# Turning x on VectorE by 32 x 32 blocks, with the product q (k^T v) on quarters of TensorE's columns

## The chip, the cores and the metric

One core of one Trainium2 chip. The metric is the device time of one execution in microseconds (us), lower is better. PE is TensorE's matmul side, DVE is VectorE, ACT is ScalarE.

## The reference

Linear attention with a norm over each head, then a two-layer network with a squared relu:

```python
kv  = einsum('bhsd,bhse->bhde', k, v)          # 8 batches, 8 heads, 576 positions, 64 wide
out = einsum('bhsd,bhde->bhse', q, kv)
x   = out / sqrt(mean(out*out, -1) + 1e-6) * g_norm
x   = x.transpose(0, 2, 1, 3).reshape(4608, 512)
h   = x @ w_in                                 # 512 x 2048
g   = s * maximum(h, 0)**2 + b
y   = g @ w_out                                # 2048 x 512
```

All of it is f32. The two large products dominate. They need x with its features on the partitions, that is, turned.

## The kernel before

The 4608 rows are 36 chunks of 128 tokens, four chunks to a unit, nine units. The large products run by one level of Strassen's scheme (line 84 is their one helper), in slots of 16 matmul records. While the second product of unit u runs, the attention of unit u + 1 is slipped in between its slots, a piece at a time. For each chunk: q is turned (`turn`), multiplied by the block-diagonal k^T v (`product`), normed (`norm`), and turned again (`turn_x`). The pieces that the change touches:

```python
def kv_product(b):                       # k^T v of one batch: 72 matmuls on 64 x 64 quarters
    ...
    nc.tensor.matmul(ps[r][l * HB : l * HB + HB, i, :],
                     lhsT=kv[rows, 0, l, j, :], rhs=kv[rows, 1, l, j, :], ...)
    ...
    nc.scalar.copy(to, ps[r][ls])        # out of PSUM into the block diagonal bd_kv

def product():
    for p in range(NP):                  # NP = 4 pairs of heads
        if b == b1:                      # a chunk of one batch: all 128 columns
            matmul(ps[:, p, :], st["qT"][:, p, :], bd_kv[b % 2][:, p, :], True, True)
            continue
        for s in range(2):               # 4 of 36 chunks: a half of the columns for each batch
            half = slice(s * HB, s * HB + HB)
            nc.tensor.matmul(ps[half, p, :], lhsT=st["qT"][:, p, half],
                             rhs=bd_kv[(b + s) % 2][:, p, :], start=True, stop=True)
    ...

def turn_x():
    ps = ps_t.tile([P, NP, P], FP32, name="xT_ps", tag="t")
    for p in range(NP):
        nc.tensor.transpose(ps[:, p, :], st["xn"][:, 2 * p : 2 * p + 2, :], ident)
    ...
    nc.scalar.activation(xT[u][:, :, j * P : j * P + P], ps, AF.Copy, scale=g_col)
```

## Time and profile before

| | before |
|---|---|
| median | 994.3 us |
| span of the profiled run | 992.7 us |
| TensorE busy | 98% |
| VectorE, ScalarE busy | 46%, 21% |
| turning x (four transposes a chunk, 36 chunks) | 2% of the chain that ended last |

TensorE sets the time nearly everywhere, so what counts is how long its instruction stream is. Durations in the profile are latencies of a pipeline that overlap: a record of the large products lasts 379 ns, but the next one starts 216 ns after it. So the length of the stream is read from starts. The prediction below shows the lines.

### The profile page before, as it was taken

How to read it: one execution, taken by the hardware profiler on the slowest of the kernel's cores; microseconds unless marked ns; L12 is line 12 of the kernel's file. 1: busy time of each engine (PE TensorE's matmuls, PEld its weight loads, DVE VectorE, ACT ScalarE, POOL GpSimd, SP SyncE). 2: the span in 40 equal slices, each digit the busy share in tenths (PEclk: the TensorE clock that was granted, in tenths of full speed). 3: DMA queues.
4: the chain of work that ended last, by engine and by line, in shares of the span. 5: the costliest groups of instructions: out<-in, count | busy, mean ns of one | idle time of the engine just before them, and what ended most of it. 6: DMA issues, size and time to landing. Idle time of an engine off the chain costs nothing.

```text
span 992.7 us, 13559 instructions
## 1 busy us (share of the span) xinstructions
PE 970.0 (98%) x5826; PEld 854.0 (86%) x5826; DVE 452.8 (46%) x741; ACT 203.7 (21%) x350; POOL 3.9 (0%) x12
## 2 busy tenths in 40 slices
PE   4999999999999999999999999999999999999998
PEld 4788788888888888888888888888888888888887
DVE  2789548452445334533345244523453344334431
ACT  2674131212121212121211212121212111112100
POOL 1000000000000000000000000000000000000000
PEclk9999999999999999999999999999999999999999
DMA  9679728522551345132543255226113340323033
GB/s 263 202 267 243 234 75 233 139 85 96 159 139 51 119 135 124 54 137 74 151 112 126 65 149 139 85 85 173 40 42 127 87 126 1 130 74 137 1 127 85
DMA packets 74028, 121.47 MB, mean 122 GB/s; under 512 B 41584, under 2 KB 47728, under 8 KB 66672
## 3 DMA queue, kind: packets, MB, share of 16 engines
q1 hardware_dynamic: 72208, 119.16, 39.9%
q10 hardware_dynamic: 1632, 1.44, 0.6%
q8 instruction: 46, 0.75, 0.3%
q14 instruction: 14, 0.11, 0.0%
q0 software_dynamic: 128, 0.00, 0.0%
HBM read 103.81 MB, written 16.78 MB: 121 GB/s over the span
## 4 chain that ended last, share of the span: by engine, by line
PE 95%; DVE 3%; DMA 1%; ACT 0%; issue 0%; SPq 0%; ACTq 0%; DVEq 0%
PE x_ps L84 51%; PE y_ps L84 30%; PE z_ps L84 8%; PE kv_ps L297 2%; PE qT_ps L327 2%; PE xT_ps L372 2%; DMA kv_sb<-in_v_dram 1%; DVE ws L186 1%; PE x_ps L345 0%; DVE xs L186 0%; DVE a L183 0%; DVE ws L183 0%; SPq L96 0%; DVE xn L363 0%; DVE a L426 0%
## 5 line engine op out<-in xcount | busy, mean ns | idle before, releaser
L84 PE MATMUL x_ps<-w_sb,a 128*128 128x256 f32 x768 | 172.3, 379 | 0.0
L84 PEld LDWEIGHTS x_ps<-w_sb,a 128*128 128x128 f32 x768 | 144.3, 190 | 18.9 <-issue 0.2
L84 PE MATMUL y_ps<-w_sb,a 128*128 128x256 f32 x640 | 143.4, 379 | 0.0
L84 PEld LDWEIGHTS y_ps<-w_sb,a 128*128 128x128 f32 x640 | 119.4, 190 | 15.2 <-issue 0.2
L84 PE MATMUL x_ps<-xs,ws 128*128 128x256 f32 x512 | 121.1, 379 | 1.3 <-DVE ws L186 1.1
L469 ACT COPY r<-x_ps 128x512 f32<-128x512 f32 x96 | 56.3, 586 | 315.4 <-PE x_ps L84 307.4
L84 PE MATMUL y_ps<-xs,wb 128*128 128x256 f32 x512 | 121.0, 379 | 0.0
L84 PEld LDWEIGHTS x_ps<-xs,ws 128*128 128x128 f32 x512 | 97.1, 190 | 15.2 <-issue 1.4
L84 PEld LDWEIGHTS y_ps<-xs,wb 128*128 128x128 f32 x512 | 97.3, 190 | 13.2
L183 DVE TENSOR_TENSOR a<-y_ps,r 128x512 f32<-128x512 f32 x64 | 44.0, 688 | 122.1 <-ACT r L469 122.1
L84 PE MATMUL x_ps<-xT,wa 128*128 128x256 f32 x384 | 91.1, 384 | 0.0
L84 PEld LDWEIGHTS x_ps<-xT,wa 128*128 128x128 f32 x384 | 74.1, 193 | 10.4
L426 DVE SCALAR_TENSOR_TENSOR a<-a 128x512 f32<-128x512 f32 x96 | 66.4, 692 | 3.3
L541 DVE SCALAR_TENSOR_TENSOR or<-x_ps,s_col,b_row 128x256 f32<-128x256 f32 x52 | 25.0, 482 | 91.4 <-PE x_ps L84 87.2
L84 PE MATMUL x_ps<-xT,ws 128*128 128x256 f32 x256 | 61.1, 381 | 0.0
L84 PE MATMUL z_ps<-xT,wa 128*128 128x256 f32 x256 | 60.5, 379 | 0.0
L84 PE MATMUL x_ps<-w_sb,s 128*128 128x256 f32 x256 | 57.8, 380 | 0.0
L356 DVE TENSOR_REDUCE ss<-xn 128x8 f32<-128x512 f32 x36 | 24.6, 684 | 71.8 <-ACT xn L354 71.8
L502 DVE TENSOR_TENSOR a<-a 128x512 f32<-128x512 f32 x32 | 22.2, 692 | 76.0 <-ACT a L501 76.0
L84 PEld LDWEIGHTS z_ps<-xT,wa 128*128 128x128 f32 x256 | 48.6, 190 | 6.6
L84 PEld LDWEIGHTS x_ps<-xT,ws 128*128 128x128 f32 x256 | 48.1, 190 | 6.7
L84 PEld LDWEIGHTS x_ps<-w_sb,s 128*128 128x128 f32 x256 | 47.6, 190 | 6.1 <-issue 0.2
(96 smaller groups left out, 835.7 us busy)
## 6 DMA issues: line engine op xcount, KB each, us to landing
w_sb<-w SPq DMA_DIRECT2D x56, 1024.0 KB, 4.9
out_dram<-o SPq DMA_DIRECT2D x72, 128.0 KB, 2.3
q_sb<-in_q_dram SPq DMA_DIRECT2D x70, 128.0 KB, 5.8
kv_sb<-in_k_dram SPq DMA_DIRECT2D x30, 288.0 KB, 5.3
kv_sb<-in_v_dram SPq DMA_DIRECT2D x30, 288.0 KB, 6.7
w_raw<-in_moe_w_in_dram SPq DMA_DIRECT2D x8, 1024.0 KB, 5.4
w_raw<-in_moe_w_out_dram SPq DMA_DIRECT2D x8, 1024.0 KB, 5.0
w<-w_up SPq DMA_DIRECT2D x3, 1024.0 KB, 7.1
```

Source lines behind the costliest of these rows:

```text
L84: nc.tensor.matmul(o, lhsT=lhsT, rhs=rhs, start=start, stop=stop, skip_group_check=True)
L183: nc.vector.tensor_tensor(out=o, in0=a, in1=b, op=ALU.add)
L186: nc.vector.tensor_tensor(out=o, in0=a, in1=b, op=ALU.subtract)
L297: nc.tensor.matmul(ps[r][l * HB : l * HB + HB, i, :], lhsT=kv[rows, 0, l, j, :], rhs=kv[rows, 1, l, j, :], start=(j == 0), stop=(j == R - 1),)
L327: nc.tensor.transpose(ps[:, p, :], q_in[c][:, 2 * p : 2 * p + 2, :], ident)
L356: nc.vector.reduce_sum(st["ss"], st["xn"], axis=mybir.AxisListType.X)
L372: nc.tensor.transpose(ps[:, p, :], st["xn"][:, 2 * p : 2 * p + 2, :], ident)
L426: nc.vector.scalar_tensor_tensor(t, t, 0.0, t, ALU.max, ALU.mult)
L469: nc.scalar.copy(st[name], src)
L502: nc.vector.tensor_mul(t, t, t)
L541: nc.vector.scalar_tensor_tensor(o, ps, s_col, other, ALU.mult, ALU.add)
```

## The change

The intent is to take the four transposes of x in each chunk off TensorE and give them to VectorE, which has room. VectorE's transpose turns only blocks of 32 x 32 (the page is named in the prediction). The new layout takes each block to stay on its 32 partitions. So the product writes each block of 32 tokens of a head pair to the quarter of the partitions on which its features shall lie, and k^T v's columns, w_in's rows and g_norm are put in an order that fits. ScalarE then scales by g_norm in place.

```diff
@@ load of w_in
-  in_=src.rearrange("(c p) n -> p c n", p=P)[...]
+  in_=src.rearrange("(p c) n -> p c n", c=KC)[...]
@@ g_norm: 8 small loads in place of 2
-  for l in range(2): ... g_col[l * HB : l * HB + HB, :] <- g_norm "(p o) -> p o"
+  for h in range(H): ... g_col[h * e : h * e + e, :] <- g_norm "(e c) -> e c"
@@ kv_product: v is streamed in the new order of columns
-  ps[r][l * HB : l * HB + HB, i, :],
+  ps[r][l * HB : l * HB + HB, i, :].rearrange("p (c e) -> p c e", c=KC),
-  rhs=kv[rows, 1, l, j, :],
+  rhs=kv[rows, 1, l, j, :].rearrange("p (e c) -> p c e", c=KC),
@@ product: quarters of the columns, neighbours on different quarters
+  for w in range(4):
+      for p in range(NP):
+          nc.tensor.matmul(ps[32 * p : 32 * p + 32, w, :],
+                           lhsT=st["qT"][:, p, 32 * w : 32 * w + 32],
+                           rhs=bd_kv[(b if w < 2 else b1) % 2][:, p, :], start=True, stop=True)
@@ norm: writes runs of 16 elements
@@ turn_x
-  4 x nc.tensor.transpose(...); nc.scalar.activation(xT[...], ps, AF.Copy, scale=g_col)
+  nc.vector.transpose(out=to, in_=st["xn"]...)
+  every second chunk: 4 x nc.scalar.activation(to[:, i], to[:, i], AF.Copy, scale=g_col[:, i : i + 1])
```

More of the change, by code (lines that the diff above doesn't have):

```diff
@@ L136, in load_w @@
                 out=dst.rearrange("p (c n) -> p c n", c=KC),
-                in_=src.rearrange("(c p) n -> p c n", p=P)[:, :, f * n : f * n + 2 * n],
+                in_=src.rearrange("(p c) n -> p c n", c=KC)[:, :, f * n : f * n + 2 * n],
             )
@@ L266 @@
         nc.gpsimd.memset(t, 0.0)
-    g_col = const.tile([P, 1], FP32, name="g_col")
-    for l in range(2):
+    g_col = const.tile([P, KC], FP32, name="g_col")
+    for h in range(H):
+        e = D // KC
         nc.gpsimd.dma_start(
-            out=g_col[l * HB : l * HB + HB, :], in_=g_norm.rearrange("(p o) -> p o", o=1)
+            out=g_col[h * e : h * e + e, :], in_=g_norm.rearrange("(e c) -> e c", c=KC)
         )
@@ L338, in product @@
                 ps = ps_a.tile([P, NP, P], FP32, name="x_ps", tag="x")
-            for p in range(NP):
-                if b == b1:
-                    matmul(ps[:, p, :], st["qT"][:, p, :], bd_kv[b % 2][:, p, :], True, True)
-                    continue
-                for s in range(2):
-                    half = slice(s * HB, s * HB + HB)
+            for w in range(4):
+                for p in range(NP):
                     nc.tensor.matmul(
-                        ps[half, p, :],
-                        lhsT=st["qT"][:, p, half],
-                        rhs=bd_kv[(b + s) % 2][:, p, :],
+                        ps[32 * p : 32 * p + 32, w, :],
+                        lhsT=st["qT"][:, p, 32 * w : 32 * w + 32],
+                        rhs=bd_kv[(b if w < 2 else b1) % 2][:, p, :],
                         start=True,
@@ L362, in norm @@
             nc.vector.reciprocal(inv, rms)
+            shape = (P, H, KC, D // KC)
             nc.vector.tensor_tensor(
-                out=st["xn"], in0=st["x"], in1=inv.unsqueeze(2).to_broadcast((P, H, D)),
+                out=st["xn"].rearrange("p h d -> p (h d)").rearrange(
+                    "p (c h e) -> p h c e", c=KC, h=H
+                ),
+                in0=st["x"].rearrange("p h (c e) -> p h c e", c=KC),
+                in1=inv.unsqueeze(2).unsqueeze(3).to_broadcast(shape),
                 op=ALU.mult,
@@ L369, in turn_x @@
             u, j = divmod(c, 4)
-            ps = ps_t.tile([P, NP, P], FP32, name="xT_ps", tag="t")
-            for p in range(NP):
-                nc.tensor.transpose(ps[:, p, :], st["xn"][:, 2 * p : 2 * p + 2, :], ident)
             if j == 0:
                 xT[u] = xp.tile([P, KC, 2 * TB], FP32, name="xT", tag="xT")
-            nc.scalar.activation(xT[u][:, :, j * P : j * P + P], ps, AF.Copy, scale=g_col)
+            to = xT[u][:, :, j * P : j * P + P]
+            nc.vector.transpose(
+                out=to, in_=st["xn"].rearrange("p h d -> p (h d)").rearrange("p (c x) -> p c x", c=KC)
+            )
+            if j % 2 == 1:
+                to = xT[u][:, :, j * P - P : j * P + P]
+                for i in range(KC):
+                    nc.scalar.activation(
+                        to[:, i], to[:, i], AF.Copy, scale=g_col[:, i : i + 1]
+                    )
         return turn, product, norm, turn_x
```

## The prediction

> **What bounds the kernel now.** I read the page's first two parts, then the chain that ended last, then the groups by form, and last the timeline of TensorE around the lines that the change touches.
>
> ```profile
> PE 970.0 (98%) x5826; PEld 854.0 (86%) x5826; DVE 452.8 (46%) x741; ACT 203.7 (21%) x350; POOL 3.9 (0%) x12
> ...
> PE 95%; DVE 3%; DMA 1%; ACT 0%; issue 0%; SPq 0%; ACTq 0%; DVEq 0%
> PE x_ps L84 51%; PE y_ps L84 30%; PE z_ps L84 8%; PE kv_ps L297 2%; PE qT_ps L327 2%; PE xT_ps L372 2%; DMA kv_sb<-in_v_dram 1%; DVE ws L186 1%; PE x_ps L345 0%; DVE xs L186 0%; DVE a L183 0%; DVE ws L183 0%; SPq L96 0%; DVE xn L363 0%; DVE a L426 0%
> ```
>
> TensorE is the bound in every stage but the first 35 us; VectorE is busy 46% and ScalarE 21%, so both have room on average. The part to be removed, the turning of x (L372), is about 2% of the chain. Its groups, with the other attention work on TensorE:
>
> ```profile
> L372 PE MATMUL xT_ps<-ident,xn 128*128 128x128 f32 x144 | 21.7, 273 | 1.9 <-DVE xn L363 1.7
> L297 PE MATMUL kv_ps<-kv_sb 64*64 64x64 f32 x1152 | 21.0, 231 | 11.4 <-DMA kv_sb<-in_v_dram 11.4
> L345 PE MATMUL x_ps<-bd_kv,qT 128*64 128x128 f32 x64 | 4.4, 279 | 0.0
> ```
>
> The durations (273 ns) are latencies of a pipeline; the cost is the spacing of starts. That is read in TensorE's timeline: first a chunk of 128 tokens that lies over two batches (product on halves of the columns), then an ordinary one:
>
> ```profile
> 328.85 0.60 PE L372 MATMUL xT_ps<-ident,xn 128*128 128x128 f32 x4
> 329.38 1.09 PE L345 MATMUL x_ps<-bd_kv,qT 128*64 128x128 f32 x16
> 330.41 3.72 PE L84 MATMUL y_ps<-w_sb,a 128*128 128x256 f32 x16
> ...
> 337.86 0.60 PE L372 MATMUL xT_ps<-ident,xn 128*128 128x128 f32 x4
> 338.29 1.06 PE L84 MATMUL x_ps<-bd_kv,qT 128*128 128x128 f32 x8
> 339.19 0.60 PE L84 MATMUL x_ps<-w_sb,s 128*128 128x256 f32 x2
> ```
>
> The reader is to see starts: ordinary, four transposes take 338.29 - 337.86 = 0.43 us and eight records of the product (four f32 matmuls, two records each) 0.90. Both are 0.11 us a record. The product on halves needs sixteen records of the same 128 columns, and from transposes to the next group it takes 330.41 - 328.85 = 1.56 against 339.19 - 337.86 = 1.33, and the group behind it takes 3.72 instead of the 3.62 that the same form takes elsewhere. So halves do run two at a time, and going into and out of that mode costs 0.23 + 0.10 = 0.33 us.
>
> The product k^T v already runs on 64 x 64 quarters:
>
> ```profile
> 276.28 1.89 PE L84 MATMUL x_ps<-xT,wa 128*128 128x256 f32 x8
> 278.10 2.33 PE L297 MATMUL kv_ps<-kv_sb 64*64 64x64 f32 x144
> 280.36 1.99 PE L84 MATMUL x_ps<-xT,ws 128*128 128x256 f32 x8
> ```
>
> 144 records in 280.36 - 278.10 = 2.26 us are 0.0157 us each. A 256-column record takes 0.216 (16 in 3.45 by the chain), so 64 columns alone would take 0.054: four tiles run at once.
>
> **What the Trainium skill says.** "TensorE: Matmul & The Clock Gate", Part 3: small matmuls whose outputs lie in different groups of 32 partitions run concurrently. The trace agrees for two column tiles and for four 64 x 64 tiles (above); four tiles of 32 columns are not in it. "TensorEngine Tiling (Array Packing)", Key Properties: a change of tiling mode drains TensorE. The trace agrees: 0.33 us there and back. "SBUF — State Buffer", Specifications: SBUF has lines of 16 bytes and wants at least two hits on a line for full bandwidth. No instruction of this trace streams with a stride, so nothing confirms or refutes it. "VectorE: DVE Perf Modes", The three transpose paths: VectorE turns only blocks of 32 x 32, to SBUF. The trace of before has none.
>
> **The change part by part.** There are 36 chunks; 4 run in the opening, 32 beside the large matmuls, 4 of these on halves already.
>
> 1. Removed from TensorE: four transposes a chunk, 32 x 0.436 = 14.0 us on the path (all 36: 15.7). This is the most that can be won: 1.6%.
>
> 2. The product now has sixteen matmuls, 32 records, on four column groups, in an order in which neighbours differ in group. Serial, 32 x 0.109 = 3.5 us; four at a time, 0.87, as before. Into and out of the mode: 0.33 by the halves, say 0.35. For 28 ordinary chunks that is new, 28 x 0.35 = 9.8 us. The 4 on halves pay it already: about 0.
>
> 3. Steady sum: -14.0 + 9.8 = -4.2 us. Most of the gain goes back to mode changes.
>
> 4. k^T v streams v with a stride of 4 f32, 16 bytes, so each element lies in a line of its own. If the stream keeps its rate: 0. If it halves, the 1.95 us of each batch (2.26 less some 0.3 of mode change) doubles: seven batches and the half of the first that isn't hidden by its loads, 7.4 x 1.95 = 14.4 us, all on the path.
>
> 5. VectorE gets one transpose of 128 x 512 a chunk. No duration is shown; I take the 0.69 us of its other one-element-a-cycle operations of that size (rows of L356, L363), 36 x 0.69 = 25 us, to 48% busy. The norm writes runs of 16 elements, at the same cost. ScalarE exchanges one 128 x 512 eviction (688 ns) for two in-place scalings of 128 x 256; a scaled 128 x 256 took 474 ns (L574), so about +0.26 us a chunk and a block of four of some 1.8 us per two chunks. Both hide in steady units: a chunk's product has two slots of 3.45 us till the next one.
>
> 6. In the first unit's second half products follow each other after one slot (5.2 us apart). There the block of four scalings stands in ScalarE's queue before the square of the next product; by adding up the queue I get VectorE's norm done 5.8 us after the slot's end where TensorE wants the bank at 5.1: one stall of 0.7 us.
>
> 7. The opening is a chain of latencies. The first large matmul started at 28.50, held by VectorE's copies. In the new order on VectorE two transposes of 0.69 stand among them, then the four scalings: the second transpose ends at 28.6, the scalings at 30.3, so +1.8 there. The next block's weights are prepared behind those and come at 35.1 against the 34.88 at which TensorE used them. The third block needs chunks 2 and 3 turned and scaled, 39.8 against 38.34: +1.5 stays.
>
> 8. g_norm is loaded in eight small DMAs instead of two. The order with its waits shows that b's load now waits for the second of them; b landed at about 12.1 us (issue at 3.93, 8.2 to landing), and VectorE's first operation waits for it. Landing at 10 for that one and some 4 to 7 us more gives 14 to 17, and VectorE is wanted at 16.4 (the copy of k^T v). I put 0.3 us. The other order of w_in's rows leaves size and number of pieces as they are: 0.
>
> Sum without the stride's cost: 994.3 - 4.2 + 0.7 + 1.6 + 0.3 = 992.7. With it: 1007.
>
> **Rivals.** (a) The stride costs. For it: the skill's line rule, every element on its own line. Against: f32 streams at one element per two array cycles (0.216 us for 256), half the rate of access that a 2-byte type would ask, and the 64 x 64 mode already reads two streams from each row without loss. I give it 0.4, and 1003 to 1010 us. (b) The four column groups don't run at once, for instance since f32 takes two records and both need the same tile. For it: nothing but that no such mode is in the trace. Against: halves and quarters do, with f32. It would cost 36 x 1 to 2.6 us, 1030 to 1085: 0.05. (c) Mode changes cost nothing here, since the removed transposes stood on the other side: 983. Against it, L345 shows the cost each of the four times with transposes before it: 0.05. (d) VectorE or ScalarE become the bound in the steady part: they would have to run over 3.4 us late in a slot; 48% and some 22% busy speak against it.
>
> **Range and chances.** The case without stride cost stands at 992.7, with 988 to 997 for the opening and the mode change; the other at 1007. The middle of the whole is a little over the first: 995. A range of 988.5 to 1009 holds both. Faster by over 2% would mean under 974.4, 20 us, more than the 15.7 that are taken away: 0.01. Slower by over 2% means over 1014, which needs (b) or a stride that costs more than half the rate: 0.06.
>
> **What would show it.** The product's line, formerly two forms, should have 1152 records, starts from product to next group 0.9 + 0.23 us apart in all chunks, and the next group lengthened by 0.10. kv_ps should keep 2.26 us per batch; at 4.2 rival (a) is right. The transposes of VectorE should be about 0.69 us, VectorE about 48% busy. The first large matmul should start near 30.3 us instead of 28.5. Wrong would be: a product of 3.5 us, a wait of TensorE for ScalarE's scaling or for xn in units after the first, or VectorE's first operation after 17 us.

## The result, and the profile after

The changed kernel takes 1002.0 us at the median (1001.6 to 1002.5, 4 runs) against 994.3 (994.1 to 994.6, 4 runs): ratio 1.0077, 95% interval 1.006 to 1.0095. It is within 2%, but clear of noise: the change loses 8 us, though it takes 14 us of work off TensorE.

The page of the changed kernel, engine totals and chain:

```profile
PE 979.1 (98%) x6514; PEld 851.7 (85%) x6514; DVE 474.6 (47%) x777; ACT 208.7 (21%) x386; POOL 6.7 (1%) x18
...
PE x_ps L84 48%; PE y_ps L84 30%; PE z_ps L84 8%; PE x_ps L345 3%; PE kv_ps L299 3%; PE qT_ps L331 1%; DMA kv_sb<-in_k_dram 1%; DMA q_sb<-in_q_dram 1%; DVE ws L186 1%; DVE xs L186 0%; DVE a L183 0%; DVE ws L183 0%; DVE a L437 0%; PE y_ps L345 0%; DVE wb L186 0%
```

The line of xT_ps is gone from the chain; kv_ps has gone from 2% to 3% of it, and the product has a line of its own with 3%. Neither VectorE nor ScalarE has become busy. The groups that take these places, by form:

```profile
L345 PE MATMUL x_ps<-bd_kv,qT 128*32 128x128 f32 x1088 | 37.3, 278 | 1.6 <-DVE qT L334 1.1 <-DVE xn L364 0.5
L299 PE MATMUL kv_ps<-kv_sb 64*64 64x64 f32 x1152 | 35.8, 293 | 10.2 <-DMA kv_sb<-in_v_dram 10.2
```

kv_ps has the same count of records as before, 1152, and 35.8 us busy where it had 21.0. TensorE's timeline around one batch's k^T v:

```profile
277.81 1.89 PE L84 MATMUL x_ps<-xT,wa 128*128 128x256 f32 x8
279.63 4.41 PE L299 MATMUL kv_ps<-kv_sb 64*64 64x64 f32 x144
283.97 2.00 PE L84 MATMUL x_ps<-xT,ws 128*128 128x256 f32 x8
```

From 279.63 to 283.97 are 4.34 us; before it was 2.26. And around an ordinary chunk's product:

```profile
329.32 3.62 PE L84 MATMUL x_ps<-w_sb,a 128*128 128x256 f32 x16
332.87 1.08 PE L345 MATMUL x_ps<-bd_kv,qT 128*32 128x128 f32 x32
333.88 3.72 PE L84 MATMUL y_ps<-w_sb,a 128*128 128x256 f32 x16
337.44 0.60 PE L331 MATMUL qT_ps<-ident,q_sb 128*128 128x128 f32 x4
```

32 records take 333.88 - 332.87 = 1.01 us where 8 took 0.90, so four column groups do run at once. But the group in front takes 332.87 - 329.32 = 3.55 where sixteen such records take 3.45, and the one behind is lengthened from 3.62 to 3.72: 0.11 + 0.10 + 0.10 = 0.31 us that an ordinary chunk did not pay before.

To see where all of the span went, I summed the intervals from the start of each matmul record to the start of the next, charged to the earlier one (us; the k^T v of the first batch falls into the first 40 us):

| charged to | before | after | e1 | e7 |
|---|---|---|---|---|
| turning x | 14.25 | 0 | 0 | 0 |
| k^T v, 7 batches | 15.87 | 30.37 | 15.85 | 16.31 |
| product | 29.09 | 32.35 | 32.35 | 30.14 |
| turning q | 14.03 | 14.14 | 14.14 | 14.38 |
| large products | 874.66 | 878.90 | 879.77 | 874.91 |
| first 40 us, and the end | 44.82 | 44.93 | 44.92 | 44.76 |
| span | 992.7 | 1000.7 | 987.0 | 980.5 |

(e1 and e7 are experiments below. The cut at 40 us falls into a group, so the last two rows can trade some records of 0.22 us.) Between before and after: -14.25 for turning, +14.50 for k^T v, +3.26 for the product, +4.24 for the large products, +0.2 for the rest: +8.0, the difference of the spans.

### The profile page after: what moved, and what is told of

Its sections match the earlier page's. It is cut to its first block, busy times and chain, and to the rows that moved or that the text cites. A ratio compares the mean times of both kernels' runs of the same rounds, so it can differ in the third digit from the quotient of the medians. Undisturbed runs are those within 1.5% of the kernel's fastest.

```text
span 1000.7 us, 15059 instructions
## 1 busy us (share of the span) xinstructions
PE 979.1 (98%) x6514; PEld 851.7 (85%) x6514; DVE 474.6 (47%) x777; ACT 208.7 (21%) x386; POOL 6.7 (1%) x18
## 4 chain that ended last, share of the span: by engine, by line
PE 94%; DVE 3%; DMA 2%; issue 0%; SPq 0%; ACT 0%; DVEq 0%; ACTq 0%
PE x_ps L84 48%; PE y_ps L84 30%; PE z_ps L84 8%; PE x_ps L345 3%; PE kv_ps L299 3%; PE qT_ps L331 1%; DMA kv_sb<-in_k_dram 1%; DMA q_sb<-in_q_dram 1%; DVE ws L186 1%; DVE xs L186 0%; DVE a L183 0%; DVE ws L183 0%; DVE a L437 0%; PE y_ps L345 0%; DVE wb L186 0%
```

## The experiments

The theory: streaming v with a stride of 16 bytes halves the rate of k^T v and costs 14.5 us; the changes into and out of the column mode cost 0.31 us in each of 28 chunks, 8.7; together they eat the 14.25 that the removal of the transposes brings. The rivals: that quarters or VectorE's transposes carry the loss; that any pattern other than contiguous slows the stream; that the cost at the products is of the work and not of the change of mode.

**e1: v contiguous, the order made in the eviction.** The changed kernel with (cut to its core; the output pattern and VectorE's copies for the first batch are changed alike)

```diff
-  rhs=kv[rows, 1, l, j, :].rearrange("p (e c) -> p c e", c=KC),
+  rhs=kv[rows, 1, l, j, :],
+  to = to.rearrange("p i (c e) -> p i c e", c=KC)
+  ev = ps[r][ls].rearrange("p i (e c) -> p i c e", c=KC)
-  nc.scalar.copy(to, ps[r][ls])
+  nc.scalar.copy(to, ev)
```

> The changed kernel with v streamed contiguously; its columns are put in the new order when k^T v is copied out of PSUM instead. Theory (the 16-byte stride of the moving operand costs 14.5 us): kv_ps back to 2.26 us per batch, 1002.0 - 14.5 = 987.5, which is faster than the kernel before by 7 us. Rival (the product on quarters or the VectorE transposes carry the loss): it stays near 1002. If the permuted eviction is slow on ScalarE it is still hidden, since the copies are off the chain.

Correct, 987.7 us (986.7 to 988.8, 5 runs), ratio 0.9930 to before (0.9917 to 0.9944). The group of kv_ps is what it was before:

```profile
L299 PE MATMUL kv_ps<-kv_sb 64*64 64x64 f32 x1152 | 21.0, 231 | 11.0 <-DMA kv_sb<-in_v_dram 11.0
```

So all of the 14.5 us hang on how v is read, and without them the kernel is 7 us faster than before. (Some 1.6 of these 7 us are a pause that the kernel before has and e1 has not; see e2.) The eviction reads PSUM with the stride now, and ScalarE's copies took 259 ns in the mean where they took 260: the order costs nothing there.

**e2, e3, e4: the kernel before, with only v's stride.** In each, v is streamed with a stride of 4, 2 or 8 f32 and the order is undone in the eviction, so the results are right (the diff is cut in the same way):

```diff
-  rhs=kv[rows, 1, l, j, :],
+  rhs=kv[rows, 1, l, j, :].rearrange("p (e c) -> p c e", c=4),      # e3: c=2, e4: c=8
+  ev = ps[r][ls].rearrange("p i (c e) -> p i e c", c=4)             # undone
```

> The kernel before with only v streamed with a stride of 4 f32 (16 bytes), and the order undone in the eviction, so the result is right. Theory: kv_ps 4.3 us per batch and 994.3 + 14.5 = 1008.8. Rival (kv_ps was slow in the changed kernel by something else, such as the loads' timing): 994.

> The kernel before with v streamed with a stride of 2 f32 (8 bytes), undone in the eviction. If what counts is two hits on a 16-byte line: kv_ps stays 2.26 us per batch and the time 994.3. Rival (any step over one element, or the two-dimensional pattern itself, costs): kv_ps 3.3 to 4.3 us, 1001 to 1009.

> The kernel before with v streamed with a stride of 8 f32 (32 bytes), undone in the eviction. If each 16-byte line that is opened for one element costs the same: as with 4, kv_ps 4.3 us per batch, 1007. If the cost grows with the distance: more, 1020 and up.

All correct. Stride 4: 1006.9 us (4 runs), ratio 1.0127 (1.0113 to 1.0141). Stride 2: 994.5 (4 runs), 1.0001 (0.9987 to 1.0014). Stride 8: 1006.9 (one run). The group of kv_ps, in the order 2, 4, 8, each from its own run:

```profile
L297 PE MATMUL kv_ps<-kv_sb 64*64 64x64 f32 x1152 | 21.1, 230 | 10.9 <-DMA kv_sb<-in_v_dram 10.9
```

```profile
L297 PE MATMUL kv_ps<-kv_sb 64*64 64x64 f32 x1152 | 35.8, 293 | 10.8 <-DMA kv_sb<-in_v_dram 10.8
```

```profile
L297 PE MATMUL kv_ps<-kv_sb 64*64 64x64 f32 x1152 | 36.2, 295 | 10.5 <-DMA kv_sb<-in_v_dram 10.5
```

A stride of 8 bytes is free, 16 bytes costs 14.7 us of busy time more, and 32 bytes hardly more than that. It is the step that the line rule cited in the prediction leads one to expect: two elements on a 16-byte line are enough, one is not. The pattern's being two-dimensional, which e3 has too, is not the cause. All of this is f32 on 64 x 64 quarters; no run strides the operand of a matmul on the whole array. The time of e2 rose by 12.7 us and not by 14.5. In its trace a pause is missing that the trace of before has in the first unit:

```profile
114.09 0.92 PE L84 MATMUL x_ps<-w_t,a 128*128 128x256 f32 x3
116.47 1.78 PE L84 MATMUL x_ps<-w_t,a 128*128 128x256 f32 x7 [1.46 <-issue]
```

TensorE stands idle for 1.5 us in the middle of a group (1.84 us from start to start where 0.22 is usual, so 1.6 are lost), waiting for nothing that the profile shows. e3 has a shorter one at the same record (1.2 lost); the changed kernel and the traces of all other experiments have none. With it, 14.5 - 1.6 = 12.9 fits the 12.7.

No experiment was made on the pause, but the packets in the traces point at the instructions' own loads. Queue q8 brings instructions in blocks of 16 KB, 46 of them before and 51 after, in step with TensorE's 5826 and 6514 matmul records. Before, such a block starts at 114.12 us and TensorE goes on at 116.47; in e3 they are at 113.59 and 115.90, so both go on 2.3 us after the block's start. In e2 and e4 the same block starts at 114.04 and 113.12, while the slower k^T v still runs (until 116.36 and 115.3), and there is no pause. In the changed kernel no block starts between 97.02 and 117.71. So TensorE may have run out of instructions behind the quick k^T v; this fits and is not shown.

**e5 and e5b: the kernel before with all products on halves.** This leaves the transposes where they were and measures the change of mode alone:

```diff
-  if b == b1:
+  if False:
       matmul(ps[:, p, :], ...)
```

> The kernel before with all products on halves of the columns, as it has them for 4 of 36 chunks. Nothing else changes, so it measures the mode change alone. By the prediction's 0.33 us a chunk: 28 x 0.33 = +9.2, 1003.5. By what the changed kernel's intervals give (about 7.0 us for 28 chunks): 1001. If mode changes were free: 994.3.

The first try gave a wrong result (1001.2 us, ratio 1.0070, 1.0056 to 1.0083): I had overlooked that the second half then reads `bd_kv[(b + s) % 2]`, the other batch's matrix. Put right (`b if s == 0 else b1`):

> The run e5_halves put right: there the second half of the tokens read the k^T v of the other batch, so its result was wrong. Theory: correct, and the same time, 1001, with L345 and what is around it 0.31 us longer per chunk; if the wrong matrix had brought a wait of its own, less than 1001.

Correct, 1001.6 us (one run), so the wrong matrix had not changed the time. Its timeline around an ordinary chunk:

```profile
329.44 0.60 PE L372 MATMUL xT_ps<-ident,xn 128*128 128x128 f32 x4
329.97 1.09 PE L345 MATMUL x_ps<-bd_kv,qT 128*64 128x128 f32 x16
330.99 3.72 PE L84 MATMUL y_ps<-w_sb,a 128*128 128x256 f32 x16
```

0.53 from the transposes to the product where the ordinary chunk of before had 0.43, 1.02 to the next group against 0.90, and 3.72 against 3.62: 0.32 us, the same as with quarters. Over 28 chunks 9.0, less the pause of 1.6 that this trace lacks too, gives 7.4; measured 1001.6 - 994.2 = 7.4.

**e6: e1 with neighbours on the same quarter.**

```diff
-  for w in range(4):
-      for p in range(NP):
+  for p in range(NP):
+      for w in range(4):
```

> e1 with the two loops of the product exchanged, so that four neighbours go to the same column group. If neighbours must differ in group to run at once (matmuls start in program order): some 3.5 us a chunk in place of 0.9, 32 to 36 x 2.6 = +83 to +94 us, 1071 to 1081. If TensorE looks further ahead: 988.

Correct, 1033.2 us (one run): both numbers missed, though the direction was that of the first. One product:

```profile
326.71 3.62 PE L84 MATMUL y_ps<-w_sb,a 128*128 128x256 f32 x16
330.26 2.46 PE L347 MATMUL x_ps<-bd_kv,qT 128*32 128x128 f32 x32
332.65 3.72 PE L84 MATMUL x_ps<-w_sb,a 128*128 128x256 f32 x16
```

2.39 us in place of 1.01. Strictly one after the other, 32 records of 0.109 would be 3.5. If each started in program order, only the last record of a quarter could run beside the first of the next, an estimate of 29 x 0.109 = 3.2. The single records in the trace show more overlap: the first record of a quarter lasts 297 ns and those behind it some 273, and such a first record starts at 330.73, just after the fifth of the eight on the quarter before it (330.72; told apart by their spacing of 0.11), whose last three start later, at 330.83, 330.94 and 331.05. So TensorE looks ahead, not far. The order that the change chose, neighbours on different quarters, is worth 1.4 us a chunk.

**e7: e1 with two products back to back.** If the cost at the products is that of going into and out of the mode, two chunks can share it. The product of every second chunk gets a bank of the pool that the transposes of x no longer use:

```diff
-  product = [whole(*steps) for steps in zip(product, norm)]
+  pair = [[product[i], product[i + 1], norm[i], norm[i + 1]] for i in (0, 2)]
-  ps = ps_a.tile([P, NP, P], FP32, name="x_ps", tag="x")
+  pool, tag = (ps_t, "t") if c % 2 else (ps_a, "x")
+  ps = pool.tile([P, NP, P], FP32, name="x_ps", tag=tag)
@@ after which slot of a unit's second product which pieces of the attention stand
-  3: [product[0]], 4: [turn[1]], 5: [turn_x[0], product[1]], 6: [turn[2]],
-  7: [turn_x[1], product[2]], 8: [turn[3]], 9: [turn_x[2], product[3]], 11: [turn_x[3]]
+  3: [turn[1]], 4: pair[0], 6: [turn[2], turn_x[0]], 7: [turn[3], turn_x[1]],
+  8: pair[1], 10: [turn_x[2]], 11: [turn_x[3]]
@@ the first unit in the same way: 6: [turn[0], turn[1], kv_product], 7: pair[0], ..., 10: pair[1], 11: [turn_x[2]], 12: [turn_x[3]]
```

> e1 with the products of two chunks one right behind the other from the second unit on (32 chunks), so that one way into and out of the column mode serves two. Theory (0.31 us for a way in and out, and a 0.6 us stall in the first unit that the new places of the products avoid): 16 x 0.31 + 0.6 = 5.6 us less than e1, so 982.1. Rival (the cost is of each product, not of the change of mode): 987.7, or more if the later turning makes the sums of x late.

Correct, 982.3 us (982.2 to 982.5, 4 runs), ratio 0.9881 (0.9864 to 0.9897): the best of all kernels here, by 12 us against before and by 20 against the change.

```profile
333.58 3.62 PE L84 MATMUL x_ps<-w_sb,s 128*128 128x256 f32 x16
337.13 1.95 PE L348 MATMUL x_ps<-bd_kv,qT 128*32 128x128 f32 x64
339.01 3.72 PE L84 MATMUL x_ps<-w_sb,s 128*128 128x256 f32 x16
```

64 records in 1.88 us, and again 3.55 in front and 3.72 behind: two products pay some 0.3 once. The rival, that the cost is of each product, falls.

## Why the prediction was right or wrong

It put the range right; its middle, 995, is 7 us low. That the time lies in the range says little of the mechanism, since the range was made to hold two cases, 992.7 without and 1007 with a cost of the stride, and the case that it held for the likelier one did not come. The other is 5 us high, and 1002.0 lies just under the 1003 to 1010 that it gave for that case: the opening (1.5), the mode changes (1.1) and g_norm's loads (0.3) cost less than predicted, and the pause of 1.6 us went. By its own steps:

1. Removed transposes: 14.0 us; measured 14.25. Right.
2. Quarters: the four at a time were right (1.01 us). The way into and out of the mode was read from the chunks on halves as 0.33, put at 0.35, and measured 0.31: 8.7 instead of 9.8. e5b finds the same 0.32 with halves and with the transposes in their place; e7 shows that two products share it, so that it is of the mode and not of the product. Rivals (b), groups not at once, and (c), mode changes free, are refuted.
3. So the steady sum without k^T v, predicted as -4.2, is -14.25 + 8.7 = -5.6.
4. The stride. This is where the middle failed: not in the size, which was 14.4 for halving and is 14.5, but in the weight. The prediction gave the stride's cost a chance of only 0.4, though the line rule that it cited spoke for it; it set against the rule that the 64 x 64 mode reads two streams from each row without loss. That says nothing of a stride, and no line of its trace did. e2 shows the full halving, e3 that two elements on a line suffice, as the line rule has it. Its rival (a) is what happened.
5. VectorE's transposes took 703 ns instead of 0.69 us, the scalings 498 ns instead of 474, VectorE stands at 47%. Right, and hidden in steady units: after the opening, TensorE's only wait that the kernel before has not is the stall of step 6, so rival (d) falls too.

```profile
L378 DVE STREAM_TRANSPOSE xT<-xn 128x512 f32<-128x512 f32 x36 | 25.2, 703 | 0.2
L384 ACT ACTIVATE xT<-xT,g_col 128x256 f32<-128x256 f32 x72 | 30.7, 498 | 55.8 <-DVE xT L378 55.8
```

6. The stall in the first unit: predicted 0.7 us. The changed kernel has it, at the place named and once:

```profile
135.20 3.62 PE L84 MATMUL x_ps<-w_dn,a 128*128 128x256 f32 x16
139.36 1.08 PE L345 MATMUL x_ps<-bd_kv,qT 128*32 128x128 f32 x32 [0.54 <-DVE xn L364]
```

   4.16 us from start to start against 3.55 with only the change of mode: 0.6. In e7 it is gone.
7. The opening: predicted +1.5 (the prediction's sum adds 1.6, a slip of 0.1); the sum over the first 40 us grew by 0.1. The lines of the changed kernel (of all engines, cut):

```profile
29.07 5.88 PE L84 MATMUL x_ps<-xT,wa 128*128 128x256 f32 x16
...
34.78 3.62 PE L84 MATMUL y_ps<-xT,wb 128*128 128x256 f32 x16
...
37.55 1.71 ACT L384 ACTIVATE xT<-xT,g_col 128x256 f32<-128x256 f32 x4 [1.97 <-DVE xT L378]
...
38.24 3.62 PE L84 MATMUL x_ps<-xT,wa 128*128 128x256 f32 x16
```

   The third group starts at 38.24 while the four scalings run until 39.26. I had let it wait for all four; each of its matmuls waits only for the block of features that it reads: the scalings end at 38.06, 38.46, 38.86 and 39.26, and the matmuls that wait for them start at 38.24, 38.67, 39.10 and 39.53. Besides, in this execution the second half of k and v had landed a microsecond earlier (k^T v's second part started at 12.67 instead of 13.72). Kernels that do not touch the loads vary as much: the share of k^T v in the first 40 us was 7.45 in before, 7.49 in e2 and 6.38 in e3. So the opening's small differences are not laid to the change.
8. The loads of g_norm: VectorE's first operation that waits for b started at 14.68 instead of 12.22, and VectorE was wanted at 15.54. Later, as predicted, and no cost.

Put together: -14.25 + 8.7 + 14.5 + 0.6 + 0.1 would be +9.6; the pause of 1.6 us that before has and the changed kernel has not brings it to +8.0. That last term the prediction could not have.

## What to carry to other kernels

When a layout has to be permuted, do it where the data is evicted anyway rather than in TensorE's moving operand: here 16 bytes of stride in f32 nearly doubled the time of the 64 x 64 matmul stream, while ScalarE's copy did the same permutation for nothing. And before splitting TensorE's columns, count the changes of mode: some 0.3 us here for going in and coming out together took away more than half of what the removed transposes gave, until two products shared one change.

## What the Trainium skill lacked or had wrong

- "SBUF — State Buffer", Specifications, gives the rule of two hits on a 16-byte line without the size of the penalty. Here, for f32 as the moving operand on 64 x 64 quarters: k^T v of a batch 2.26 us with stride 1 and the same busy time with stride 2 (21.0 and 21.1 us in all), 4.34 us with stride 4, and no more to speak of with stride 8 (35.8 and 36.2 us in all). The page's note on cachelines adds that one can stride for free as far as "4 fp32"; taken as a stride of 4, that is wrong here: 2 was free, 4 was not.
- "TensorEngine Tiling (Array Packing)", Key Properties, says that a change of mode drains TensorE, without a duration: 0.31 us for going in and coming out, the same for 64 and 32 columns, a third of it within the product and the rest in the large groups before and behind.
- "TensorE: Matmul & The Clock Gate", Part 3, calls the matmuls strictly first-in first-out. With neighbours on the same quarter (e6) 32 records took 2.39 us, where starts in program order would give about 3.2 by the estimate above, and the first record of a quarter started before the last three of the quarter ahead of it.
- No page has a measured duration for VectorE's transpose of f32: 128 x 512 took 703 ns.
